# Summing the four classes of a long convolution's products on GpSimd in f32, so that an inverse transform takes 16 matmuls in place of 32

## The chip, the cores and the metric

The kernel runs on one core of a Trainium2 chip. The metric is the device time of one execution in microseconds (us); lower is better. A core has a matrix engine (TensorE, PE in the profile, with its weight loads as PEld), a vector engine (VectorE, DVE), a scalar engine (ScalarE, ACT), a general engine (GpSimd, POOL), and SyncE (SP), which here only issues DMA transfers. Each engine works through its own instruction queue in order; an instruction at the head that must wait holds all that stands behind it. Transfers run on 16 DMA engines. Operands lie in SBUF; matmul results lie in PSUM, which GpSimd does not read in this kernel.

## The reference, cut to what matters

Two independent halves share the kernel, and their outputs lie side by side.

```
a: for each of 64 segments of 32 rows: attention over 8 memory rows + 32 rows, 32 heads of 128,
   the memory rows of a segment come out of the segment before        (Wq, Wk, Wv, Wo: 4 x 8 MB)
b: P  = exp(dt * A * l),  l = 0..2047                                   (1024 channels, N = 128)
   K  = real(sum over n of C * P * dt * B)                              (1024 x 2048)
   Kf = rfft(K padded to 4096);  Uf = rfft(u padded to 4096)
   y  = irfft(Uf * Kf)[0:2048] + u * Dskip
output = concat(a, b)
```

The change lies in the last part of b: the product of the two spectra and the inverse transform back to 2048 points, scaled, with `u * Dskip` added.

## The kernel before, in words

Part b comes first (0 to about 642 us of the profiled execution), part a after it (to 1990 us). Part a goes through the 64 segments one after another; most of its weights lie in SBUF by then, and the rest is streamed from memory in every segment through four slots of 512 KB. Some of the resident weights are loaded while part b still runs, each when the SBUF that it takes is free; these loads are the `next(resident)` calls in part b, and they stand in SP's queue between the loads of part b.

Up to about 420 us, part b makes the filter K (exponentials, sines, products) and transforms the input u forward. The rows of K go through memory (`Kd`). Those transfers that are left when this stage ends are issued from GpSimd's queue (`for f_ in late: f_(gp)`; the issue is at line 1063): 40 of them, and they stand in the queue ahead of all that GpSimd is given later.

Then comes the stage of the change. The 2048 points are split into four classes by their index modulo 4; the transform's matrices (cosines and sines) are 128x128 blocks. The work is cut into 16 blocks `b`: quarter `dq = b // 4` of the channels (256 each) and row block `kc = b % 4` of the frequencies. For each block:

- TensorE makes the filter's spectrum of the next block, 40 matmuls (`spectrum`, line 1207), into PSUM tiles `hps` (two for a block, three buffers from block 4 on).
- VectorE multiplies it by the input's spectrum: four instructions of 128x1024 f32 (`times_u`, line 1360), one input in SBUF and one in PSUM, into `Y` and `Z`. The two input halves `uq` (`wq` in the trace) are loaded by SP with `load_u`, each when `times_u` of the block before is through with it.
- `pointwise` then does Y -= Z and Y += Z with the parts crossed (lines 1416 and 1417) and the sum and difference of the two halves of Y (line 1419, two instructions of 128x1024, f32 in, bf16 out) into `Bt[:, kc]`. `Bt` holds all four `kc` of one quarter; it has two places, one for even and one for odd quarters.
- In blocks 0 to 2 VectorE also multiplies matrices by amplitudes (`weighted`, line 1191), before and after the four instructions of `pointwise`; the spectra of the next block wait for them.

From block 4 on, two inverse transforms of the quarter before are run behind each block (`inverses(2)`). An inverse gives 2x128 points of one class `r = c // 4` for 256 channels: for each of two output blocks, four `kc` and cosine and sine, two matmuls of 128x128 by 128x256 (line 1469), one for each half of `Bt`. That is 32. Where the class needs a half with a minus sign, the matmul takes a negated copy `mn` of its matrix `MI`, which ScalarE makes ahead of time (`negated`, line 1435). ScalarE scales the sum into `yb` (line 1484); VectorE multiplies u by Dskip and adds `yb` (lines 1489 and 1490: 128x512 bf16, two inputs in SBUF). These endings are run by `end()`, behind `times_u` of the next block. ScalarE then issues the store.

After block 15 the last quarter's eight inverses remain. Three are begun over `kc` 0 to 2 (`inverse_begin`), then all eight are ended one by one, each followed by `next(resident)`, and with the first by twelve of them.

The framework keeps the order in which each engine's instructions are written and puts in the waits: a write waits until all earlier reads of the same bytes are over. GpSimd's queue in this stage holds: the 40 issues of `Kd`; in block 2 one multiplication on 4 partitions and some small fills (lines 1550 to 1553); in block 4 the constants of part a, 36 selections (line 231) and some more; in block 10 one copy (line 1688).

Of the kernel before, what the change touches and what calls it, by code (L numbers as in the profile page):

```python
# [10 lines left out]
BF16 = mybir.dt.bfloat16  # L11
F32 = mybir.dt.float32
I32 = mybir.dt.int32
I16 = mybir.dt.int16
ALU = mybir.AluOpType
ACT = mybir.ActivationFunctionType
# [682 lines left out]
def part_b(ctx, tc, u, A_re, A_im, B_re, B_im, C_re, C_im, log_dt, Dskip, out_b, ahead, copies, residents, first_state):  # L699
# [5 lines left out]
    DH, DQ = 512, 256  # L705
    v, sc, gp, pe, sy = nc.vector, nc.scalar, nc.gpsimd, nc.tensor, nc.sync
# [46 lines left out]
    with tc.tile_pool(name="b_par", bufs=1) as par, tc.tile_pool(name="b_parh", bufs=2) as parh, \  # L753
# [112 lines left out]
        low, neg = (par.tile(sh, BF16, name=n_) for n_ in ("low", "neg"))  # L866
# [441 lines left out]
    for f in range(16):  # L1308
# [14 lines left out]
        for word in ORDER if f else FIRST:  # L1323
            nm, r = word.rstrip("'"), f - word.endswith("'")
# [26 lines left out]
    def make(kc, n):  # L1351
        for _ in range(n):
            next(made[kc])
# [3 lines left out]
    def times_u(s_, Y, Z, n_):  # L1357
        us = uq[n_].rearrange("p (a c d) -> p a c d", a=2, c=2)
        for i, t_ in ((1, Z), (0, Y)):
            v.tensor_tensor(out=t_[:, n_], in0=us[:, :, i, :].unsqueeze(2).to_broadcast([128, 2, 2, DQ]), in1=s_[n_][0], op=ALU.mult)  # L1360
# [28 lines left out]
    ctx1.close()  # L1389


    mnp = ctx.enter_context(tc.tile_pool(name="b_mn", bufs=2))
    iv = ctx.enter_context(tc.tile_pool(name="b_iv", bufs=2))
    bp = ctx.enter_context(tc.tile_pool(name="b_B", bufs=1))
    Dsk = const.tile([128, D], BF16, name="Dsk")
# [3 lines left out]
    bp0 = ctx2.enter_context(tc.tile_pool(name="b_B0", bufs=1))  # L1399
# [4 lines left out]
    MI = [pool.tile([128, 2, 2, 4, 128], BF16, name="MI", tag="MI%d" % i) for i in range(8)]  # L1404
# [3 lines left out]
    def pointwise(b, s_):  # L1408
        kc, Bt = b % 4, Bs[b // 4]
        Y, Z = (pw.tile([128, 2, 2, 2, DQ], F32, name=nm, tag=nm)[:] for nm in "yz") if b else first  # L1410
        if b:
            for n_ in range(2):
                times_u(s_, Y, Z, n_)
        yield
        Yc, Zc = (t_.rearrange("p a b c d -> p (a b) c d") for t_ in (Y, Z))
        v.tensor_tensor(out=Yc[:, :, 0, :], in0=Yc[:, :, 0, :], in1=Zc[:, :, 1, :], op=ALU.subtract)
        v.tensor_tensor(out=Yc[:, :, 1, :], in0=Yc[:, :, 1, :], in1=Zc[:, :, 0, :], op=ALU.add)
        for j, op in ((0, ALU.add), (1, ALU.subtract)):
            v.tensor_tensor(out=Bt[:, kc, j], in0=Y[:, 0], in1=Y[:, 1], op=op)

    NIV, UU = 3, 7
    unsent = []
# [4 lines left out]
        sy.dma_start(out=uu[:], in_=u_v[r][:, mc:mc + 2, DQ * dq:DQ * dq + DQ])  # L1427
        return uu

    def negated(c):  # L1430
        neg = (None, (1, 2), (0, 2), (0, 1))[c // 4]
        mn = None
        if neg:
            mn = mnp.tile([128, 2, 2, 4, 128], BF16, name="mn", tag="mn")
            sc.activation(out=mn[:, :, neg[0]:neg[1]], in_=MI[c // 2][:, :, neg[0]:neg[1]], func=ACT.Copy, scale=-1.0)
        return neg, mn

    ready = []

    def inverses(n):  # L1440

        for _ in range(n):
            dq, c = todo.pop(0)
            if not ready:
                ready.append(negated(c))
            inverse(dq, c, nxt.pop(0), *ready.pop(0))
            if len(todo) >= NIV:
                nxt.append(load_inverse(*todo[NIV - 1]))

    early = {}  # L1450

    def inverse_begin(dq, c, yp):
        ready.append(negated(c)) if len(ready) * 2 <= c else None
        early[dq, c] = yp
        products_back(yp, dq, c, *ready[c // 2], range(3))

    def products_back(yp, dq, c, neg, mn, kcs):
        r, Bt = c // 4, Bs[dq]
        j = r % 2
        for b in range(2):  # L1460
            for kc in kcs:
                if kc == 3 and b == 1 and c % 4 == 2:
                    pe.matmul(yp[:, b, :], lhsT=l4[:, r, :], rhs=w4[:, DQ * dq:DQ * dq + DQ], start=False, stop=False, skip_group_check=True)
                for cs in range(2):

                    g_cs = cs if j == 0 else 1 - cs
                    minus = neg is not None and neg[0] <= cs < neg[1]
                    for half, m_, c_ in ((0, MI[c // 2], cs), (1, mn if minus else MI[c // 2], g_cs)):
                        pe.matmul(yp[:, b, :], lhsT=m_[:, b, cs, kc, :], rhs=Bt[:, kc, j, half, c_, :], start=(kc == 0 and cs == 0 and half == 0),  # L1469
                                  stop=(kc == 3 and cs == 1 and half == 1), skip_group_check=True)  # L1470

    def inverse(dq, c, uu, neg, mn):
        r, mc = c // 4, c % 4
        d = slice(DQ * dq, DQ * dq + DQ)
        if (dq, c) in early:
            yp = early[dq, c]
            products_back(yp, dq, c, neg, mn, range(3, 4))
        else:
            yp = ps_y.tile([128, 2, DQ], F32, name="yp", tag="yp")[:]
            products_back(yp, dq, c, neg, mn, range(4))  # L1480
        if todo and not ready:
            ready.append(negated(todo[0][1]))
        yb = iv.tile([128, 2, DQ], BF16, name="yb", tag="yb", bufs=2)
        sc.activation(out=yb[:], in_=yp, func=ACT.Copy, scale=float(2.0 / PLEN))
        while unsent:
            unsent.pop(0)()

        def ending():
            v.tensor_tensor(out=uu[:], in0=uu[:], in1=Dsk[:, d].unsqueeze(1).to_broadcast([128, 2, DQ]), op=ALU.mult)
            v.tensor_tensor(out=uu[:], in0=uu[:], in1=yb[:], op=ALU.add)  # L1490
            unsent.append(lambda: sc.dma_start(out=out_v[r][:, mc:mc + 2, d], in_=uu[:]))
        endings.append(ending)
# [3 lines left out]
    def end():  # L1496
        while endings:
            endings.pop(0)()

    todo = [(dq, c) for dq in range(4) for c in range(0, 16, 2)]  # L1500
    nxt = []
    Bs = [None] * 4
# [6 lines left out]
    for b in range(16):  # L1509
        dq = b // 4  # L1510
        if b % 4 == 0:
            Bs[dq] = (bp0, bp)[dq % 2].tile([128, 4, 2, 2, 2, DQ], BF16, name="Bt", tag="B")
        points = pointwise(b, now)
        next(points)
        end()
        if b + 1 < 16:
            load_u(b + 1)
        if b == 0:
            ctx_p.close()
            ps_h = ctx_h.enter_context(tc.tile_pool(name="b_psh0", bufs=2, space=PSUM))  # L1520
        if b == 3:
            nxt = [load_inverse(*todo[n_]) for n_ in range(NIV)]
            ctx_h.close()
            ctx_f.close()
            ps_h = ctx.enter_context(tc.tile_pool(name="b_psh", bufs=3, space=PSUM))
            ps_y = ctx.enter_context(tc.tile_pool(name="b_psy", bufs=2, space=PSUM))
        if b + 1 < 16:
            now = []
            for n_ in range(2):
                if b < 3:  # L1530
                    if n_:
                        next(points, None)
                    weighted(b + 1, n_, amps[b + 1])
                now.append([ps_h.tile([128, 2, 2, DQ], F32, name="hps", tag="h")[:]])
                spectrum(b + 1, n_, [now[n_][0][:, half] for half in range(2)])
                if b == 0:
                    next(points, None)
                if b < 2:
                    make(b + 2, (9, 5)[n_])
        next(points, None)  # L1540
        if b < 4:
            for i in (2 * b, 2 * b + 1):
                sy.dma_start(out=MI[i][:], in_=MId[2 * i:2 * i + 2].rearrange("c p a k q -> p c a k q"))
        if b == 2:
            ks.append(load_k(1, k1[:, 0:2560], 0))
            rows4 = g0[0:4, 5120:6144]
            for i in range(4):
                sy.dma_start(out=rows4[i:i + 1, 0:D], in_=Kd[640:641, :])
            sy.dma_start(out=w4, in_=u[0:4, :])
            gp.tensor_tensor(out=w4, in0=rows4[:, 0:D], in1=w4, op=ALU.mult)  # L1550
            gp.memset(l4, 0.0)
            gp.memset(l4[:, :, 127:128], float(PLEN / 2))
            gp.affine_select(out=l4[:, :, 127:128], in_=l4[:, :, 127:128], compare_op=ALU.is_ge, fill=0.0, base=0, pattern=[[1, 4], [0, 1]],
                             channel_multiplier=-1)
        for _ in range({1: 2, 2: 2, 3: 1, 4: 2, 5: 2, 6: 2, 7: 1, 11: 3, 12: 3, 13: 2, 14: 3}.get(b, 0)):
            next(resident)
        if b == 4:
            state = first_state(g0[0:8, 5120:6144], iv.tile([128, 8, 24], BF16, name="xt0", bufs=1))
            next(state)
        if b == 10:  # L1560
            state.send(ps_y.tile([128, 8, 128], BF16, name="yp", tag="yp")[:, :, 0:8])
        if b >= 4:
            inverses(2)
# [166 lines left out]
```

## Time and profile before

| what | value |
|---|---|
| time, median of three runs | 1983.08 us (1977.25 to 1986.69) |
| the profiled execution's own time | 1991.66 us |
| its span, first to last instruction | 1989.9 us (1.8 us lie around it) |
| TensorE busy | 1846.9 us, 93% of the span |
| VectorE busy | 1370.6 us, 69% |
| ScalarE busy | 949.3 us, 48% |
| GpSimd busy | 411.1 us, 21% |
| moved by DMA | 588.70 MB, mean 296 GB/s |
| mean granted TensorE clock | 0.973 of full |

The profiled execution is 8.6 us (0.4%) slower than the median of the three timed runs. Shares of busy time are means over the whole span, and the stage of the change is only 220 us of it (422 to 642 us), so the stage has to be read by itself: the views for it are the busy time by stretches, the timeline of one engine, the groups of one line or tile, and the chain of waits. In the timeline a row gives the start, the length, the engine, the line, the operation, the tiles written and read, the shapes, and how many instructions were merged into it. In the view of busy time by stretches each row gives the stretch, its length, the busy us (and number of instructions) of PE, PEld, DVE, ACT and POOL, the granted clock, the busy share of the DMA engines and GB/s. Rows of PE are pipelined: one matmul of 128x256 is shown with 273 ns, but the next one starts 0.109 us after it, so its rate is read from a merged row.

### The profile page before, as it was taken

What the parts mean: (1) busy time and instruction counts of PE and PEld (TensorE: products, weight loads), DVE (VectorE), ACT (ScalarE), POOL (GpSimd) and SP (SyncE); (2) the same over time, 40 slices, a digit from 0 to 9 for tenths busy, and PEclk for the clock granted to TensorE, in tenths of its full rate; (3) what the DMA queues carried; (4) which work ended last, traced back from release to release, by engine and by line L of the source; (5) the groups of instructions that cost most, each with busy time, mean ns of one, the idle gap of its engine ahead of it and who ended that gap; (6) DMA issues with size and microseconds to landing.
All of it is one profiled execution on the core that took longest, in us unless ns stands there. A gap on an engine that the chain in (4) does not pass through costs nothing.

```text
span 1989.9 us, 74737 instructions
## 1 busy us (share of the span) xinstructions
PE 1846.9 (93%) x32044; PEld 1134.5 (57%) x32044; DVE 1370.6 (69%) x3399; ACT 949.3 (48%) x1678; POOL 411.1 (21%) x859
## 2 busy tenths in 40 slices
PE   8799999778999799999999999999999999999999
PEld 3566666446887355555555555555555555555554
DVE  8499999858994466666666676666666666666650
ACT  8599999841223344343444444444444343434330
POOL 2254535224000111111111111111121111111120
PEclk9899999868999799999999999999999999999999
DMA  7789888757578899999999999999999999999991
GB/s 223 207 239 272 238 242 256 199 152 249 179 226 297 311 345 319 340 345 324 346 344 347 347 343 341 342 340 339 338 338 348 338 341 352 331 334 343 333 345 39
DMA packets 329350, 588.70 MB, mean 296 GB/s; under 512 B 86830, under 2 KB 202990, under 8 KB 326970
## 3 DMA queue, kind: packets, MB, share of 16 engines
q1 hardware_dynamic: 275592, 529.03, 78.3%
q10 hardware_dynamic: 45682, 29.82, 4.9%
q0 software_dynamic: 7744, 25.07, 3.5%
q8 instruction: 251, 4.11, 0.8%
q14 instruction: 81, 0.66, 0.1%
HBM read 528.25 MB, written 66.05 MB: 299 GB/s over the span
## 4 chain that ended last, share of the span: by engine, by line
PE 37%; DMA 24%; DVE 3%; issue 1%; ACT 1%; POOL 0%; ACTq 0%; POOLq 0%; SPq 0%; DVEq 0%
PE acc L404 20%; DMA wst<-WD_v 10%; PE pp L517 8%; DMA wst<-WD_o 6%; DMA wst<-WD_k 4%; DMA arena<-PKd 3%; PE pe L654 3%; PE tr L415 2%; DMA wst<-WD_q 1%; PE pv L485 1%; PE pv L489 1%; DVE arena L611 1%; PE sc L429 1%; ACT arena L611 1%; DVE arena L470 1%
## 5 line engine op out<-in xcount | busy, mean ns | idle before, releaser
L404 PEld LDWEIGHTS <-a_hT 128*32 128x32 bf16 x12352 | 329.7, 96 | 316.7 <-issue 62.6
L410 ACT CAST arena<-acc 128x512 bf16<-128x512 f32 x384 | 224.7, 585 | 402.0 <-PE acc L404 324.6
L517 PEld LDWEIGHTS <-arena 128*32 128x32 bf16 x8256 | 216.8, 97 | 86.3 <-issue 62.6
L404 PE MATMUL acc<-wst,a_hT 128*32 128x512 bf16 x2304 | 229.4, 382 | 26.0 <-DMA wst<-WD_v 17.6
L418 POOL COPY arena<-arena 128x128 bf16<-128x128 bf16 x128 | 37.3, 292 | 839.2 <-DMA arena<-PKd 278.6
L325 DVE TENSOR_SCALAR arena<-keep 128x256 int32<-128x256 int32 (+1 forms) x512 | 175.7, 395 | 31.5 <-PE acc L404 30.9
L404 PE MATMUL acc<-XM,a_hT 128*32 128x512 bf16 x2560 | 185.8, 381 | 0.0
L517 PE MATMUL pp<-W_o,arena 128*32 128x256 bf16 x3584 | 123.4, 274 | 6.9 <-DMA W_o<-in_A_Wo_dram 6.3
L444 DVE TENSOR_REDUCE a_mx<-sc 128x4 f32<-128x160 f32 (+1 forms) x192 | 71.6, 373 | 78.8 <-PE sc L432 78.8
L197 PE MATMUL pro<-XM,wsl 128*128 128x512 bf16 x512 | 122.3, 382 | 3.8 <-DVE kst L206 2.2
L448 ACT ACTIVATE sc<-sc 128x160 f32<-128x160 f32 (+1 forms) x192 | 63.9, 333 | 124.2 <-DVE sc L445 123.9
L404 PE MATMUL acc<-W,a_hT 128*32 128x512 bf16 x1536 | 118.6, 381 | 0.0
L532 DVE COPY arena<-tr 128x512 bf16<-128x512 bf16 x64 | 27.2, 425 | 127.7 <-PE tr L415 127.7
L452 DVE TENSOR_REDUCE a_mx<-sc 128x4 f32<-128x160 f32 (+1 forms) x192 | 72.9, 379 | 55.3 <-ACT sc L448 54.9
L1252 DVE TENSOR_SCALAR nr<-ptt 128x456 f32<-128x456 int16 x128 | 80.4, 628 | 38.6 <-PE ptt L1230 35.5
L1469 PE MATMUL yp<-Bt,MI 128*128 128x256 bf16 x680 | 104.5, 273 | 0.0
L404 PE MATMUL acc<-g,a_hT 128*32 128x512 bf16 x1024 | 101.8, 380 | 0.0
L479 POOL TENSOR_TENSOR arena<-arena,a_BD 128x128 bf16<-128x128 bf16 x128 | 51.0, 399 | 229.7 <-DVE arena L462 222.7
L1244 ACT ACTIVATE E<-pa 128x648 bf16<-128x648 f32 x128 | 87.9, 713 | 16.8 <-PE pa L1236 14.2
L611 ACT CAST arena<-pp 128x128 bf16<-128x128 f32 x64 | 17.0, 265 | 164.7 <-DVE arena L611 164.7
L404 PE MATMUL acc<-wq,a_hT 128*32 128x512 bf16 x1024 | 90.8, 382 | 0.0
L517 PE MATMUL pp<-wst,arena 128*32 128x256 bf16 x1536 | 76.5, 275 | 15.2 <-DMA wst<-WD_o 13.1
(332 smaller groups left out, 4048.3 us busy)
## 6 DMA issues: line engine op xcount, KB each, us to landing
wst<-WD_v SPq DMA_DIRECT2D x256, 512.0 KB
wst<-WD_k SPq DMA_DIRECT2D x192, 512.0 KB
wst<-WD_o SPq DMA_DIRECT2D x192, 512.0 KB
wst<-WD_q SPq DMA_DIRECT2D x128, 512.0 KB
Ud<-ux POOLq DMA_DIRECT2D x16, 1024.0 KB, 7.9
wq<-Ud SPq DMA_DIRECT2D x32, 512.0 KB
wsl<-in_A_Wk_dram SPq DMA_DIRECT2D x16, 512.0 KB
wsl<-in_A_Wv_dram SPq DMA_DIRECT2D x16, 512.0 KB
```

Source lines behind the costliest of these rows:

```text
L197: nc.tensor.matmul(a[:], lhsT=w[:, kc, 128 * j:128 * j + 128], rhs=xTl[:, kc, :, :].rearrange("p s k -> p (s k)"), start=(kc == 0), stop=( ...
L325: nc.vector.tensor_scalar(out=out.bitcast(I32), in0=in_.bitcast(I32), scalar1=0, scalar2=None, op0=ALU.bitwise_or)
L404: nc.tensor.matmul(a[32 * g:32 * g + 32, o_:o_ + rhs.shape[1]], lhsT=hT[:, kc, :], rhs=rhs, start=(kc == 0), stop=(kc == KC - 1), tile_pos ...
L410: nc.scalar.copy(out=q, in_=a[:])
L444: nc.vector.tensor_reduce(out=m_, in_=x, axis=AX.X, op=ALU.max)
L448: nc.scalar.activation(out=flat(sc, i), in_=flat(sc, i), func=ACT.Exp, scale=scale)
L452: nc.vector.tensor_reduce(out=m_, in_=x, axis=AX.X, op=ALU.add)
L517: nc.tensor.matmul(po[32 * qt:32 * qt + 32, o_:o_ + rhs.shape[1]], lhsT=oT[:, h % 4, (h % 16) // 4, :], rhs=rhs, start=False, stop=(h == 3 ...
L654: nc.tensor.matmul(pe[n][:], lhsT=left[2 * b + hi // 16][:, 128 * (hi % 16):128 * (hi % 16) + 128], rhs=wo[u][:, 1024 * hh + 512 * n:1024 ...
L1244: sc.activation(out=T["E", r, e // 4][:, lo:lo + 8 * NE].rearrange("p (i c) -> p i c", i=2), in_=T.pop(("p", r, e))[:, :, 0:4 * NE], func= ...
L1252: v.tensor_scalar(out=T["n", r, e // 4][:, lo:lo + 8 * NT], in0=T.pop(("t", r, e))[:, 0:8 * NT].bitcast(I16)[:, 0:16 * NT:2], scalar1=floa ...
L1469: pe.matmul(yp[:, b, :], lhsT=m_[:, b, cs, kc, :], rhs=Bt[:, kc, j, half, c_, :], start=(kc == 0 and cs == 0 and half == 0), stop=(kc == 3 ...
```

## The change

VectorE now writes the sum and the difference of Y's halves in f32 into one tile `halves_` (8 KB a partition, one buffer, in the place where the two negated matrices lay). GpSimd makes the four classes from it with four instructions of 128x512 (f32 in, bf16 out) for each block: the first two read the sum, the last two the difference, one operand of each of these with its two rows in reverse order. `Bt` has the same size and is now indexed by class and part. An inverse takes two matmuls where it took four, 16 in all, and no negated matrix. All that ScalarE did for `mn` is gone. Nothing else is moved.

```diff
-    mnp = ctx.enter_context(tc.tile_pool(name="b_mn", bufs=2))
+    clp = ctx.enter_context(tc.tile_pool(name="b_cl", bufs=1))
+    halves_ = clp.tile([128, 2, 2, 2, DQ], F32, name="hv")
...
+        X = halves_
         for j, op in ((0, ALU.add), (1, ALU.subtract)):
-            v.tensor_tensor(out=Bt[:, kc, j], in0=Y[:, 0], in1=Y[:, 1], op=op)
+            v.tensor_tensor(out=X[:, j], in0=Y[:, 0], in1=Y[:, 1], op=op)
+        for r, op in ((0, ALU.add), (2, ALU.subtract)):
+            gp.tensor_tensor(out=Bt[:, kc, 2 * r:2 * r + 2], in0=X[:, 0, 0], in1=X[:, 0, 1], op=op)
+        gp.tensor_tensor(out=Bt[:, kc, 2:8:5], in0=X[:, 1, 0], in1=X[:, 1, 1, ::-1], op=ALU.add)
+        gp.tensor_tensor(out=Bt[:, kc, 3:7:3], in0=X[:, 1, 0, ::-1], in1=X[:, 1, 1], op=ALU.subtract)
...
-    def negated(c):
-        neg = (None, (1, 2), (0, 2), (0, 1))[c // 4]
...
-            sc.activation(out=mn[:, :, neg[0]:neg[1]], in_=MI[c // 2][:, :, neg[0]:neg[1]], func=ACT.Copy, scale=-1.0)
...
                 for cs in range(2):
-
-                    g_cs = cs if j == 0 else 1 - cs
-                    minus = neg is not None and neg[0] <= cs < neg[1]
-                    for half, m_, c_ in ((0, MI[c // 2], cs), (1, mn if minus else MI[c // 2], g_cs)):
-                        pe.matmul(yp[:, b, :], lhsT=m_[:, b, cs, kc, :], rhs=Bt[:, kc, j, half, c_, :], start=(kc == 0 and cs == 0 and half == 0),
-                                  stop=(kc == 3 and cs == 1 and half == 1), skip_group_check=True)
+                    pe.matmul(yp[:, b, :], lhsT=MI[c // 2][:, b, cs, kc, :], rhs=Bt[:, kc, 2 * r + cs, :], start=(kc == 0 and cs == 0),
+                              stop=(kc == 3 and cs == 1), skip_group_check=True)
...
-            Bs[dq] = (bp0, bp)[dq % 2].tile([128, 4, 2, 2, 2, DQ], BF16, name="Bt", tag="B")
+            Bs[dq] = (bp0, bp)[dq % 2].tile([128, 4, 8, DQ], BF16, name="Bt", tag="B")
```

More of the change, by code (lines that the diff above doesn't have):

```diff
@@ L1428, in load_inverse @@
         return uu
-    def negated(c):
-        neg = (None, (1, 2), (0, 2), (0, 1))[c // 4]
-        mn = None
-        if neg:
-            mn = mnp.tile([128, 2, 2, 4, 128], BF16, name="mn", tag="mn")
-            sc.activation(out=mn[:, :, neg[0]:neg[1]], in_=MI[c // 2][:, :, neg[0]:neg[1]], func=ACT.Copy, scale=-1.0)
-        return neg, mn
-    ready = []
     def inverses(n):
@@ L1443, in inverses @@
             dq, c = todo.pop(0)
-            if not ready:
-                ready.append(negated(c))
-            inverse(dq, c, nxt.pop(0), *ready.pop(0))
+            inverse(dq, c, nxt.pop(0))
             if len(todo) >= NIV:
@@ L1452, in inverse_begin, with products_back @@
     def inverse_begin(dq, c, yp):
-        ready.append(negated(c)) if len(ready) * 2 <= c else None
         early[dq, c] = yp
-        products_back(yp, dq, c, *ready[c // 2], range(3))
-    def products_back(yp, dq, c, neg, mn, kcs):
+        products_back(yp, dq, c, range(3))
+    def products_back(yp, dq, c, kcs):
         r, Bt = c // 4, Bs[dq]
-        j = r % 2
         for b in range(2):
@@ L1464, in products_back, with inverse @@
                 for cs in range(2):
-                    g_cs = cs if j == 0 else 1 - cs
-                    minus = neg is not None and neg[0] <= cs < neg[1]
-                    for half, m_, c_ in ((0, MI[c // 2], cs), (1, mn if minus else MI[c // 2], g_cs)):
-                        pe.matmul(yp[:, b, :], lhsT=m_[:, b, cs, kc, :], rhs=Bt[:, kc, j, half, c_, :], start=(kc == 0 and cs == 0 and half == 0),
-                                  stop=(kc == 3 and cs == 1 and half == 1), skip_group_check=True)
-    def inverse(dq, c, uu, neg, mn):
+                    pe.matmul(yp[:, b, :], lhsT=MI[c // 2][:, b, cs, kc, :], rhs=Bt[:, kc, 2 * r + cs, :], start=(kc == 0 and cs == 0),
+                              stop=(kc == 3 and cs == 1), skip_group_check=True)
+    def inverse(dq, c, uu):
         r, mc = c // 4, c % 4
@@ L1476, in inverse @@
             yp = early[dq, c]
-            products_back(yp, dq, c, neg, mn, range(3, 4))
+            products_back(yp, dq, c, range(3, 4))
         else:
             yp = ps_y.tile([128, 2, DQ], F32, name="yp", tag="yp")[:]
-            products_back(yp, dq, c, neg, mn, range(4))
-        if todo and not ready:
-            ready.append(negated(todo[0][1]))
+            products_back(yp, dq, c, range(4))
         yb = iv.tile([128, 2, DQ], BF16, name="yb", tag="yb", bufs=2)
```

## The prediction

> **What bounds the kernel now.** First the page, for the size of the stage. It has 1024 matmuls of line 1469 (680+248+88+8 in the groups). Then the busy time by stretches (stretch, us, PE, PEld, DVE, ACT, POOL, clock, DMA share, GB/s):
>
> ```profile
> 475.00:500.00 25.00, 25.00 (x227) 21.84 (x226) 24.48 (x27) 7.99 (x8) 9.01 (x28) 1.00 0.86 277
> 575.00:608.00 33.00, 33.00 (x299) 28.64 (x296) 29.99 (x36) 11.40 (x13) 0.00 (x0) 1.00 0.71 215
> 608.00:622.00 14.00, 12.80 (x113) 10.63 (x112) 3.05 (x9) 4.35 (x7) 0.00 (x0) 1.00 0.98 349
> 622.00:642.00 20.00, 19.29 (x185) 15.39 (x182) 5.48 (x13) 8.48 (x9) 0.00 (x0) 1.00 0.99 323
> ```
>
> To be seen: up to 608 PE is full, but DVE is at 91 to 98% beside it; from 608 PE is nearly full, and DMA is full as well. Next, one block's timeline of DVE, with PE's row beside it:
>
> ```profile
> 523.31 2.36 DVE L1419 TENSOR_TENSOR Bt<-y 128x1024 bf16<-128x1024 f32 x2
> 525.59 1.22 DVE L1360 TENSOR_TENSOR z<-wq,hps 128x1024 f32<-128x1024 f32 x1
> ...
> 530.11 0.42 DVE L1489 TENSOR_TENSOR uu<-uu,Dsk 128x512 bf16<-128x512 bf16 x1
> ...
> 531.93 0.43 DVE L1490 TENSOR_TENSOR uu<-uu,yb 128x512 bf16<-128x512 bf16 x1 [0.53 <-ACT yb L1484]
> 532.28 1.22 DVE L1416 TENSOR_TENSOR y<-y,z 128x1024 f32<-128x1024 f32 x1
> ```
> ```profile
> 523.74 6.71 PE L1469 MATMUL yp<-Bt,MI 128*128 128x256 bf16 x60
> ```
>
> A matmul takes (6.71-0.27)/59 = 0.109 us. The starts of line 1416 are 10.93 us apart in the first four blocks (477.11 to 520.85), where DVE never waits, and 11.69 in the next seven (to 602.69), where it waits about 0.5 to 0.9 for `yb`, so for PE. The mean is 125.58/11 = 11.42. DVE's own floor is 10.93: halving PE's part cannot take more than 0.5 us from a block.
>
> Last, GpSimd's queue, which gets new work, and how its work goes together with DVE's:
>
> ```profile
> 420.24 1.77 POOL L1063 DMA_DIRECT2D Kd<-KxT  x3 [34.59 <-ACT XM L1160]
> ...
> 442.65 0.55 POOL L1063 DMA_DIRECT2D Kd<-KxT  x1 [2.34 <-issue]
> ...
> 458.59 1.07 POOL L1063 DMA_DIRECT2D Kd<-KxT  x2 [0.64 <-issue]
> 466.95 2.22 POOL L1550 TENSOR_TENSOR k<-g,k 4x1024 bf16<-4x1024 bf16 x1 [7.28 <-DMA k<-in_B_u_dram]
> ...
> 471.72 12.07 POOL L231 TENSOR_SCALAR_AFFINE_SELECT a_mask<-a_mask 32x24 bf16<-32x24 bf16 x36
> ```
> ```profile
> L992 POOL TENSOR_TENSOR ux<-us x16: 1257/1263/1272, 87.5 to 380.1; 128x512 f32<-128x512 f32 x16
> ```
> ```profile
> L1419 DVE TENSOR_TENSOR Bt<-y x30: 1211/1222/3024, 441.0 to 606.2; 128x1024 bf16<-128x1024 f32 x30
> ```
>
> To be seen: GpSimd issues `Kd` until 459.7 and makes part a's constants from 470.3 to 485.0. The one instruction of line 1419 that took 3024 ns instead of 1222 is the one that began at 467.23, while GpSimd's 1550 ran to 469.17. So a DVE instruction with two SBUF inputs and a GpSimd instruction shut each other out. Those with one input in PSUM don't: line 1021 takes 679 to 683 ns beside GpSimd's 991 to 994.
>
> **The change, part by part.**
>
> *Removed.* 512 matmuls x 0.109 = 55.8 us of PE: 41.9 up to 608, hidden behind DVE's floor as above, and 14.0 after it. 24 negations on ScalarE (1.05 or 1.91 us each), idle over half of the stage; PE waited 1.3 us for them in all, which lies in the tail. DVE keeps its count; f32 out costs no more than bf16 (line 1416 1219 ns, line 1419 1222).
>
> *Added: GpSimd's 64 instructions.* No such one (512 elements, f32 in, bf16 out) is in the trace. Line 992 (f32 out) has 1263 ns and starts 1.2 us after its twin 991; line 900 (1024 elements, bf16 out) has 2126 at best, so 1063 for half. A reversed operand is not shown; double would be the upper end. I take 1.2, since 992 has the shape: 4.9 us for four, 4.3 to 5.1 without the reversal.
>
> *Step 1, the wait at block 1.* The halves have one buffer. GpSimd's four for block 0 stand behind the 40 issues of `Kd`. DVE comes to the sum of block 1 at 441.0, and may write only when GpSimd has read block 0's sum. The issues ended at 459.7. From 441 on DVE stands, SP's next loads wait for it, and the DMA engines have less to do. At the bare 0.55 us the 19 issues left at 442.65 would end at 453.5. I take the middle, 457, since the rows show both bursts at that pace and gaps. Then 4 x 1.22 for GpSimd (462) and 2.3 for DVE's two: 464.2, where before it was 443.4. That is +20.8 (17.4 to 23.6). Queued behind it on DVE: `weighted` of block 2, so PE's spectra, then all blocks to 15. From there to the first product of block 4 (472.46 before, 29.1 us) DVE has about 22 us of own work, up to 2 us for the spectrum of block 2, and the 6.5 us that the load of block 4 takes from its issue, of which some 2 stand out; together 26. So 3 us come back: **+18** (14 to 22).
>
> *Step 2, the constants.* They follow block 4's classes on GpSimd. Alone a selection takes 0.18 us, one each 0.25; against DVE's two-input instructions only one gets through for each (four of 1.07 to 1.24 us between 477.1 and 481.9). They end some 20 to 23 us after block 4's difference, and block 5's classes come after them; DVE wants to write block 6's sum at 20.7. **+5** (3 to 7).
>
> *Step 3, the blocks' period.* GpSimd's four begin when DVE's difference ends, run beside `times_u` (no clash), and end 5.0 us later (4.4 to 5.2). DVE comes to line 1489 after 4.44 and waits 0.56 (0 to 0.7). Period 11.5 (10.93 to 11.65) against 11.42, over 11 periods: **+1** (-5 to +3).
>
> *Step 4, the tail.* Block 15's difference ended at 607.4, PE's last matmul of the stage at 639.4: 32 us. Now PE waits 5 us for GpSimd, and has 92 matmuls left (10 us) and some 1.7 more at a lower clock: 17 us, 15 less. But the loads for part a cannot start sooner (their places come free with that difference), and DMA is full from 608 on:
>
> ```profile
> 640.00:650.00 10.00, 5.54 (x72) 2.48 (x65) 4.46 (x11) 1.40 (x3) 0.21 (x1) 0.98 0.97 334
> 650.00:660.00 10.00, 9.05 (x165) 4.33 (x158) 4.98 (x12) 5.54 (x10) 1.49 (x5) 0.85 0.80 256
> 660.00:670.00 10.00, 6.15 (x120) 3.41 (x112) 6.09 (x21) 2.27 (x6) 1.29 (x3) 0.83 0.96 354
> 670.00:680.00 10.00, 4.80 (x68) 2.30 (x64) 0.47 (x2) 0.56 (x3) 0.00 (x0) 0.50 0.97 357
> ```
>
> The PE that came early would stand still here; it already did, 25.5 of 40 us busy. Only DMA's gaps can be filled: 2.0 us at 650, 2.3 at 680 to 690 (share 0.77). **-4** (-8 to 0).
>
> *Sum:* 18+5+1-4 = +20 on the profiled 1991.7, so about 2012 there. The median lies 8.6 lower: 1983.1+20 = **2003**. The terms' bounds add up to +4 and +32; together they hardly fall that way, and I take +12 to +28 for this case, 1995 to 2011.
>
> **The rivals.**
>
> *A, not slower: `Kd` gets out in time.* Place: GpSimd's queue from 420 to 442. If the gaps between the issues (17.0 us of idle in all, 22.1 busy) are due to DVE and not to the transfers, the issues could end at 420.2+22.1 = 442.3, and the sum of block 1 waits 4 instead of 20 us. From step 1 +1 is left: 1+5+1-4 = +3, **1986**, within 0.5%. It decides from an end of the issues before about 446; each us later costs one. Against it: the longest gap (4.27 us to 432.23) has DVE idle for 2.5 of it and DMA nearly full. 0.14. [...]
>
> *B, faster: PE was the bound all through.* If GpSimd's work clashed with nothing, the queue let it by, and part a could start when PE is done, the gain would be 5 in the periods and 15 in the tail: -20, **1963**. For it: PE's 25.00 of 25. Against: DVE's floor, DMA's 0.98. 0.06.
>
> *C, slower still: the clock.* PE would have 72 matmuls, 7.9 us, in 11.5, with a gap of some 3.6. Gaps bring the clock down here: from 451.6 to 455.0 PE was busy 2.01 of 3.40, and the next 3.4 us had clock 0.50. If it stayed there, 72 x 0.218 = 15.7 us a block: +4.2 x 11 on top, **2049**. Against: 472.0 to 475.4 had 1.78 busy and clock 1.00 after it, and one low window of 3.4 us adds 1.7 to 7.9, still under 11.5. 0.04. [...]
>
> *D, slower still: reversed rows cost double.* Two of the four at 2.4: 7.3 us, so DVE waits 2.9 at line 1489, 2.4 more x 11 = +26, **2029**. Nothing in the trace shows it. 0.08.
>
> **How the numbers follow.** Forecast 0.68, A 0.14, B 0.06, C 0.04, D 0.08. 0.5% (about what a measurement of this kernel can tell from no change) is 9.9 us: faster 0.06, same 0.14, slower 0.80. The range takes in A and the forecast and leaves out B, C and most of D: 1984 to 2021.
>
> **What would show it.** A wait of some 19 us of DVE at the new sum in block 1, ended by GpSimd; a second of a few us two blocks after the constants; line 1489 waiting about half a us for GpSimd in each block; PE with gaps in the blocks, and low clock in some windows; the last matmul of the stage 17 us after the last difference; DMA full and PE waiting behind it. It is wrong if GpSimd's `Kd` ends near 442, if GpSimd's four take far from 5 us, or if part a's first segment starts earlier than DMA lets it in this forecast.

## The result, and the profile after

The changed kernel takes 2007.3 us (median; 2004.44 to 2014.13 in six runs) beside 1983.53 for the kernel before (1977.25 to 1988.87, six runs). The ratio is 1.0128 with a 95% interval of 1.0101 to 1.0155: slower, by 20 to 31 us. The prediction was 2003, in a range of 1984 to 2021.

The profiled execution of after took 2006.71 us. Its page begins:

```profile
span 2005.0 us, 73768 instructions
...
PE 1803.0 (90%) x31532; PEld 1086.9 (54%) x31532; DVE 1380.0 (69%) x3399; ACT 919.4 (46%) x1654; POOL 504.0 (25%) x923
```

PE is busy 43.9 us less than before and ACT 29.9 us less, and the time is longer: what was taken from these two did not shorten it (e5 below asks what it is worth alone). In after, lines 1417 and 1418 are Y -= Z and Y += Z, 1421 is the sum and the difference of Y's halves in f32 (`hv`), 1423 to 1425 are GpSimd's four, 1457 is the inverse's matmul, 1475 and 1476 are the endings. The busy time by stretches (columns as in the prediction) answers to the rows shown of before:

```profile
575.00:608.00 33.00, 26.70 (x219) 21.78 (x218) 32.07 (x37) 3.58 (x6) 17.35 (x14) 0.95 0.90 270
622.00:642.00 20.00, 11.30 (x68) 7.39 (x67) 15.04 (x21) 4.18 (x7) 6.88 (x5) 0.74 0.83 254
640.00:650.00 10.00, 8.03 (x82) 5.58 (x80) 0.00 (x0) 1.19 (x2) 0.00 (x0) 1.00 0.79 260
650.00:660.00 10.00, 0.00 (x0) 0.00 (x0) 3.12 (x7) 1.19 (x2) 0.00 (x0) 0.58 0.95 309
```

To be seen: in 575 to 608 PE has fallen from 33.00 of 33 to 26.70, and DVE has risen from 29.99 to 32.07. DVE is what the blocks go by now. From 650 to 660 PE does nothing at all, with DMA at 0.95.

To find the places where time came or went, take three marks in each trace: the start of line 1416's instruction in block 0 (before; 1417 after), that in block 4, that in block 15; and as an end the moment at which GpSimd's queue comes to the second wait of line 376, the copy with which it hands on to a segment of part a (693.0 us in before, 712.3 in after; the copy itself starts 2.3 and 3.0 us later). The same marks are read in each experiment (the expectation of e11 calls the last one the third segment). With that copy or the next one as the end, the differences to before change by at most 2.1 us. "Ratio" is that of the time to the kernel before on the same chip, with its interval.

| kernel | block 0 to 4 | 4 to 15 | 15 to the mark | sum | ratio |
|---|---|---|---|---|---|
| before | 54.3 | 125.6 | 90.3 | 270.2 | 1 |
| after | 71.5 | 130.7 | 88.2 | 290.4 | 1.0128 [1.0101, 1.0155] |
| e1_dve01 | 56.2 | 130.6 | 85.8 | 272.6 | 1.0007 [0.9986, 1.0027] |
| e2_dve01_const | 55.4 | 123.7 | 85.4 | 264.5 | 0.9986 [0.9965, 1.0007] |
| e3_const | 71.7 | 123.7 | 87.7 | 283.1 | 1.0089 [1.0054, 1.0124] |
| e4_all_dve | 58.1 | 146.8 | 85.8 | 290.7 | 1.0098 [1.0065, 1.0131] |
| e5_half | 54.1 | 120.4 | 87.8 | 262.4 | 0.9961 [0.9934, 0.9987] |
| e7_before_const | 54.6 | 125.6 | 90.8 | 270.9 | 1.0007 [0.9985, 1.0029] |
| e8_uu5 | 53.7 | 124.3 | 90.5 | 268.5 | 1.0008 [0.9985, 1.0030] |
| e9_kd_split | 60.4 | 130.8 | 89.7 | 280.9 | 1.0069 [1.0041, 1.0096] |
| e10_best | 55.3 | 123.7 | 93.2 | 272.3 | 1.0028 [1.0001, 1.0055] |
| e11_uu_act | 56.7 | 123.6 | 85.4 | 265.7 | 1.0004 [0.9983, 1.0025] |
| e13_before_uu_act | 56.6 | 128.0 | 94.6 | 279.2 | 1.0060 [1.0033, 1.0087] |

After against before, from the marks before rounding: +17.3, +5.2 and -2.2, so +20.3 at the mark. What follows the mark, the rest of part a, is the same instructions in all thirteen kernels, and took anything from 1282.0 to 1303.9 us in their profiled executions (before 1296.9, after 1292.7). A span of one execution is therefore no measure here, and the two columns at the right are read together: the sum says where, the ratio says how much. They agree within 6 us in every row (e3: +12.9 at the mark, 0.89% or 17.7 us in the time).

**Block 1.** DVE's timeline, then GpSimd's (start, length, then what it waited for in brackets):

```profile
457.74 4.62 DVE L1421 TENSOR_TENSOR hv<-y 128x1024 f32<-128x1024 f32 x2 [18.01 <-POOL Bt L1423]
462.29 2.01 DVE L1191 TENSOR_TENSOR XM<-XM,wq 128x1536 bf16<-128x1536 bf16 x1
```
```profile
439.51 0.55 POOL L1063 DMA_DIRECT2D Kd<-KxT  x1 [0.81 <-issue]
444.07 6.36 POOL L1063 DMA_DIRECT2D Kd<-KxT  x11 [4.00 <-issue]
451.43 3.78 POOL L1063 DMA_DIRECT2D Kd<-KxT  x7 [0.99 <-issue]
455.22 2.49 POOL L1423 TENSOR_TENSOR Bt<-hv 128x512 bf16<-128x512 f32 x2
457.66 1.26 POOL L1424 TENSOR_TENSOR Bt<-hv 128x512 bf16<-128x512 f32 x1
458.88 1.25 POOL L1425 TENSOR_TENSOR Bt<-hv 128x512 bf16<-128x512 f32 x1
```

The same two places of DVE in before, and then all of line 1421 in after (shortest, median and longest in ns):

```profile
441.00 2.36 DVE L1419 TENSOR_TENSOR Bt<-y 128x1024 bf16<-128x1024 f32 x2
443.28 0.95 DVE L1191 TENSOR_TENSOR XM<-XM,wq 128x1536 bf16<-128x1536 bf16 x1
```
```profile
L1421 DVE TENSOR_TENSOR hv<-y x30: 1211/1225/3483, 457.7 to 627.7; 128x1024 f32<-128x1024 f32 x30
```

To be seen: block 0's classes could start only when the last `Kd` was issued, at 455.21, though their input was ready at 426.5. DVE stood from 439.7 to 457.7 for them. It goes on when the sum has been read, not when all four are through; but its two then take 4.62 us instead of 2.36. The first of them is the longest of its line, 3.48 us: it runs beside 1424 and 1425 and ends 1.1 us behind them (461.2 against 460.1). The next instruction, `weighted`, takes 2.01 instead of 0.95, beside block 1's classes (line 1423, from 461.31 on).

**The constants**, GpSimd's timeline and DVE's:

```profile
503.83 14.84 POOL L231 TENSOR_SCALAR_AFFINE_SELECT a_mask<-a_mask 32x24 bf16<-32x24 bf16 x36
...
519.85 2.49 POOL L1423 TENSOR_TENSOR Bt<-hv 128x512 bf16<-128x512 f32 x2
```
```profile
522.37 2.27 DVE L1421 TENSOR_TENSOR hv<-y 128x1024 f32<-128x1024 f32 x1 [4.28 <-POOL Bt L1423]
...
525.79 2.27 DVE L1421 TENSOR_TENSOR hv<-y 128x1024 f32<-128x1024 f32 x1 [1.15 <-POOL Bt L1425]
```

Block 5's classes stand behind the 36 selections, and block 6's sum and difference behind those classes. One period between blocks is 18.49 us, where those after it are 11.22 to 11.24.

**A block in the steady state**, DVE and GpSimd:

```profile
604.08 2.36 DVE L1421 TENSOR_TENSOR hv<-y 128x1024 f32<-128x1024 f32 x2
...
610.88 0.66 DVE L1475 TENSOR_TENSOR uu<-uu,Dsk 128x512 bf16<-128x512 bf16 x1
```
```profile
605.38 3.41 POOL L1423 TENSOR_TENSOR Bt<-hv 128x512 bf16<-128x512 f32 x2 [5.35 <-DVE hv L1421]
608.75 1.27 POOL L1424 TENSOR_TENSOR Bt<-hv 128x512 bf16<-128x512 f32 x1
609.99 1.27 POOL L1425 TENSOR_TENSOR Bt<-hv 128x512 bf16<-128x512 f32 x1
```

The sum and difference end at 606.44; GpSimd's four end at 611.26, 4.8 us later, and line 1475 stretches from 0.42 to 0.66 beside the last of them.

**The tail**, DVE's timeline:

```profile
654.70 0.42 DVE L1475 TENSOR_TENSOR uu<-uu,Dsk 128x512 bf16<-128x512 bf16 x1 [14.95 <-DMA uu<-in_B_u_dram]
```

and PE's:

```profile
661.71 1.40 PE L404 MATMUL acc<-arena,a_hT 128*32 128x512 bf16 x4 [12.36 <-DVE arena L325]
```

PE's last inverse matmul ended at 646.2, 17.3 us after the last difference; before it was 32.2. What comes next is late: a row of u arrives at 654.7, and PE stands from 649.4 to 661.7. It waits for weights of part a that VectorE unpacks (line 325), and in VectorE's queue line 325 stands behind endings that wait for that row.

### The profile page after: what moved, and what is told of

It is laid out like the page before. It is cut to its first block, busy times and chain, and to the rows that moved or that the text cites. A ratio compares the mean times of both kernels' runs of the same rounds, so it can differ in the third digit from the quotient of the medians.

```text
span 2005.0 us, 73768 instructions
## 1 busy us (share of the span) xinstructions
PE 1803.0 (90%) x31532; PEld 1086.9 (54%) x31532; DVE 1380.0 (69%) x3399; ACT 919.4 (46%) x1654; POOL 504.0 (25%) x923
## 4 chain that ended last, share of the span: by engine, by line
PE 37%; DMA 25%; DVE 3%; ACT 1%; issue 1%; POOL 0%; ACTq 0%; SPq 0%; POOLq 0%; DVEq 0%
PE acc L404 21%; DMA wst<-WD_v 10%; DMA wst<-WD_o 8%; PE pp L517 8%; PE pe L654 3%; DMA arena<-PKd 2%; PE tr L415 2%; DMA wst<-WD_k 2%; DMA wst<-WD_q 2%; PE pv L485 1%; DVE arena L611 1%; PE pv L489 1%; PE sc L429 1%; ACT arena L611 1%; PE tro L617 1%
## 5 line engine op out<-in xcount | busy, mean ns | idle before, releaser
L452 DVE TENSOR_REDUCE a_mx<-sc 128x4 f32<-128x160 f32 (+1 forms) x192 | 72.9, 380 | 55.4 <-ACT sc L448 55.0
L1244 ACT ACTIVATE E<-pa 128x648 bf16<-128x648 f32 x128 | 88.0, 714 | 15.8 <-PE pa L1236 13.7
L1470 ACT ACTIVATE yb<-yp 128x512 bf16<-128x512 f32 x29 | 17.3, 597 | 159.2 <-PE yp L1457 132.6
```

The source lines that it names most:

```text
L452: nc.vector.tensor_reduce(out=m_, in_=x, axis=AX.X, op=ALU.add)
L1244: sc.activation(out=T["E", r, e // 4][:, lo:lo + 8 * NE].rearrange("p (i c) -> p i c", i=2), in_=T.pop(("p", r, e))[:, :, 0:4 * NE], func= ...
```

## The experiments

The theory after the result, **Q**: the loss is two waits in GpSimd's queue, one behind the issues of `Kd` and one behind the constants, and the classes in the other blocks cost nothing. Its rival, **L**: GpSimd's instructions and DVE's shut each other out in every block, and that is the loss. For the tail, **D**: DMA is full, so PE's early end buys little; the rival, **U**: the tail goes by the loads of u's rows (where they stand in a queue, or how early they are asked for; the expectations of e11 and e13 call it S).

**e1_dve01**: the first wait taken away, by giving GpSimd nothing to do in blocks 0 and 1.

```diff
+        eng = v if b < 2 else gp
...
-            gp.tensor_tensor(out=Bt[:, kc, 2 * r:2 * r + 2], in0=X[:, 0, 0], in1=X[:, 0, 1], op=op)
+            eng.tensor_tensor(out=Bt[:, kc, 2 * r:2 * r + 2], in0=X[:, 0, 0], in1=X[:, 0, 1], op=op)
```

> The changed kernel with the classes of blocks 0 and 1 summed by VectorE, all other blocks by GpSimd. Theory Q (the loss is waiting in GpSimd's queue: 17 us at block 1 behind the issues of Kd, 7 us at block 6 behind part a's constants): the wait of 18 us before block 1's sum is gone, VectorE has 8 x 0.6 = 4.9 us more, about half of it in its waits for PE: 2007 - 17 + 3 = 1993. Theory L (the loss is GpSimd's sums and their clashes with VectorE in every block): 2 of 16 blocks, so an eighth of 24: 2004.

Measured: 1.0007 [0.9986, 1.0027]; 17.8 us less at the mark than after. DVE's timeline, in block 1 and in block 6:

```profile
441.83 2.36 DVE L1421 TENSOR_TENSOR hv<-y 128x1024 f32<-128x1024 f32 x2
444.11 1.29 DVE L1424 TENSOR_TENSOR Bt<-hv 128x512 bf16<-128x512 f32 x2
...
508.75 2.27 DVE L1421 TENSOR_TENSOR hv<-y 128x1024 f32<-128x1024 f32 x1 [4.26 <-POOL Bt L1424]
```

The sum begins at once and in block 6 the second wait is as before. Moving 2 of 16 blocks takes nearly the whole loss away, while GpSimd goes on beside DVE in the other 14. That speaks for Q and against L. The expectation, 1993 us, is a ratio of 1.0048 and lies above the interval: at the mark the gain has the size that Q gives it, in the time it is larger, by no more than the two columns differ elsewhere.

**e2_dve01_const**: e1, and the second wait taken away too: the constants are made ahead of the `Kd` issues.

```diff
+    constants(tc, ahead)
     for f_ in late:
         f_(gp)
...
-        hT = constants(tc, ahead)
+        hT = ahead.low["hT"]
```

> As the run with blocks 0 and 1 on VectorE, and part a's constants put ahead of the issues of Kd in GpSimd's queue, where it stands idle for 34 us. Theory Q: the wait of 7 us at block 6 goes too: 1993 - 7 = 1986, so within 0.3% of the kernel before. Theory L: 2004, as without this edit.

Measured: 0.9986 [0.9965, 1.0007], not to be told from before. GpSimd's timeline shows the selections in what had been its idle time:

```profile
388.02 12.93 POOL L231 TENSOR_SCALAR_AFFINE_SELECT a_mask<-a_mask 32x24 bf16<-32x24 bf16 x36
```

All periods from block 5 on are now 11.22 to 11.24, and the time up to the mark is 26.0 us shorter than after's, 5.7 shorter than before's. Both waits are the loss; this is the best version of the change that was found.

**e3_const**: after, with the early constants alone. The diff is the one of e2, without e1's.

> The changed kernel with part a's constants put ahead of the issues of Kd, and nothing else: GpSimd sums all blocks. Theory Q (two separate waits in GpSimd's queue): block 6's wait of 7 us goes, block 1's stays: ratio to the kernel before 1.0128 less 0.0035, so 1.009. Rival (the second wait is only the first one's late effect): both waits stay, 1.0128.

Measured: 1.0089 [1.0054, 1.0124]; 7.3 us less at the mark than after. Block 1 waits 18.15 us in its timeline, as in after, and the long period is gone (11.23 us where after has 18.49). The intervals of the two times overlap, so it is the trace that tells them apart. 17.8 (e1) and 7.3 (e3) add up to 25.1, against the 26.0 of both together: the two waits are separate terms.

**e7_before_const**, the control: the early constants in the kernel before.

> The kernel before with part a's constants put ahead of the issues of Kd. GpSimd holds nothing that another engine waits for in that stage, so no theory expects anything: ratio 1.000 (0.998 to 1.002). If it is faster by 0.3%, the gain of the constants' move in the other runs says nothing on the wait.

Measured: 1.0007 [0.9985, 1.0029], +0.7 at the mark. The constants cost nothing where they are in before, and gain nothing by the move; they became a term only by GpSimd's new work behind them.

**e4_all_dve**: after, with all classes on VectorE (`eng = v` in e1's diff), so GpSimd has no part in it.

> The changed kernel with all sums on VectorE, none on GpSimd. Theory Q: no wait for GpSimd anywhere, but VectorE has 4 x 0.6 = 2.4 us more in a block: period 13.3 instead of 11.42 x 11 = +21, about +4 in blocks 0 to 3, -2 in the tail: 1983.5 + 23 = 2006, the same time as the changed kernel's by another way. Theory L: without GpSimd the clashes are gone, and it is clearly faster than the changed kernel, 1995 or less.

Measured: 1.0098 [1.0065, 1.0131]. DVE's timeline, two starts of one line in neighbouring blocks:

```profile
561.14 1.22 DVE L1417 TENSOR_TENSOR y<-y,z 128x1024 f32<-128x1024 f32 x1
...
574.56 1.22 DVE L1417 TENSOR_TENSOR y<-y,z 128x1024 f32<-128x1024 f32 x1
```

The period is 13.33 in most blocks (13.42 here), with four sums at 0.60 us each. That is 2.1 more than with GpSimd in each of the eleven periods: 23 us (146.8 against 123.7 in e2). GpSimd's sums, 1.27 us each, are better placed there than 0.60 on DVE, which has no room. So GpSimd's classes beside DVE are the cheaper way in the steady state, which is against L once more.

**e5_half**: how much PE's work was worth, by itself: the kernel before, with the second half's matmuls and the negations left out.

```diff
-                    for half, m_, c_ in ((0, MI[c // 2], cs), (1, mn if minus else MI[c // 2], g_cs)):
+                    for half, m_, c_ in ((0, MI[c // 2], cs),):
...
-            sc.activation(out=mn[:, :, neg[0]:neg[1]], in_=MI[c // 2][:, :, neg[0]:neg[1]], func=ACT.Copy, scale=-1.0)
```

> The kernel before with the matmuls of the second half of Bt and the negated matrices left out (so half of each inverse's products is missing): what the halving of the matmuls is worth alone, with nothing added. Theory of the prediction (VectorE's floor of 10.93 us a block, and a tail that ends by loads and not by PE): 5 in the blocks and 1 to 4 in the tail, 1983.5 - 8 = 1975. Rival B (PE is the bound all through): 5 and 14: 1964.

Measured: 0.9961 [0.9934, 0.9987], 7.8 us less at the mark: 5.1 in blocks 4 to 15, 2.5 after. The busy time by stretches:

```profile
550.00:575.00 25.00, 21.41 (x175) 17.26 (x173) 24.34 (x29) 2.98 (x5) 0.00 (x0) 0.93 0.92 280
...
620.00:630.00 10.00, 2.15 (x23) 0.54 (x12) 4.11 (x10) 1.19 (x2) 0.00 (x0) 0.67 1.04 376
```

In the blocks DVE is at 97%, and the periods are 10.92 to 11.02, the floor of DVE that the prediction gave; in the tail PE is busy 2.15 of 10 with DMA full. So 512 matmuls and 24 negations less, with nothing put in their place, are worth 8 us. In this kernel, halving PE's matmuls could not have given the 20 us of rival B.

**e9_kd_split**: the first wait made shorter in another way: every other issue of `Kd` goes to SP.

```diff
-    for f_ in late:
-        f_(gp)
+    for n_, f_ in enumerate(late):
+        f_((sy, gp)[n_ % 2])
```

> The changed kernel with every other one of the 40 issues of Kd given to SP; the classes stay on GpSimd. Theory Q: GpSimd's queue is free some 16 us sooner (about 439), the wait before block 1's sum shrinks from 18 us to 3 or less; SP is held some 8 to 10 us longer, and as much of it as the loads for block 1 are late comes back. Ratio to the kernel before 1.004 to 1.008 instead of 1.0128. Rival (the loss does not hang on that queue): 1.0128.

Measured: 1.0069 [1.0041, 1.0096]; 9.5 us less at the mark than after. GpSimd's timeline and then DVE's in block 1:

```profile
438.79 2.49 POOL L1423 TENSOR_TENSOR Bt<-hv 128x512 bf16<-128x512 f32 x2
```
```profile
442.46 1.22 DVE L1360 TENSOR_TENSOR z<-wq,hps 128x1024 f32<-128x1024 f32 x1 [12.41 <-DMA wq<-Ud]
...
450.31 2.36 DVE L1421 TENSOR_TENSOR hv<-y 128x1024 f32<-128x1024 f32 x2
```

Block 0's classes start 16.4 us earlier than in after (455.22), and block 1's sum waits for nothing. But from block 0 to 1 it takes 23.4 us where it took 15.6 in after and 15.8 in before: DVE waits 12.41 us for block 1's input, whose loads now stand behind twenty issues in SP's queue (issued at 436.6, where after has 423.6). The queue's length is the cause, and it moved along with the issues; e1, which moves the work out of the queue, gains 8 us more.

**e8_uu5**: the tail. e2, with the rows of u asked for five inverses ahead instead of three (`NIV, UU = 5, 7`).

> The run with blocks 0 and 1 on VectorE and the constants early, and in addition the rows of u for the inverses loaded five inverses ahead instead of three (NIV 5), so that fewer of them stand in SP's queue behind twelve loads of weights. Theory D (after the last difference DMA is full and decides when part a gets on): same as without it, ratio 0.9986, within 0.002. Theory U (the tail waits for those rows, 11.8 us of VectorE before the sixth ending): the first segment starts earlier and 4 to 6 us come back, ratio 0.996.

Measured: 1.0008 [0.9985, 1.0030]; from the last difference to the mark 85.7 us, where e2 has 80.6. The waits of SP's queue from 590 to 690 (us in all, times, longest), and one stretch:

```profile
SPq L1435 <- DMA out_dram<-uu: 21.8, 5, 9.2
```
```profile
600.00:610.00 10.00, 3.13 (x22) 2.04 (x19) 9.69 (x10) 1.79 (x3) 5.03 (x4) 0.72 0.29 82
```

With seven buffers, loads five ahead want a place whose store hasn't landed; SP stands (21.8 us in all, where e2 has 10.9), and with it all weights behind: DMA's share is 0.29, where e2 has 0.70. U expected a gain here, and D none: neither expected this loss of 5 us. It shows only that SP's queue is easily made worse.

**e10_best**: e8, and the classes of block 15 on VectorE as well, to have PE begin the last inverses sooner (`eng = v if b < 2 or b == 15 else gp`).

> As the run with NIV 5, and block 15's classes summed by VectorE too, which has nothing else to do then: 4 x 0.6 us instead of 6.4 us of GpSimd, so PE goes on 4 us earlier. Theory D: still no more, ratio 0.9986. Theory U: 4 us more on top, ratio 0.994.

Measured: 1.0028 [1.0001, 1.0055]; 88.4 us from the last difference to the mark. PE ended 16.7 us after the difference instead of 17.1 in e8, where 4 us had been expected: its wait for ScalarE's scaling (line 1472) grew from 1.36 to 2.41 us. Why it is a little worse than e8 was not found.

**e11_uu_act** and **e13_before_uu_act**: U in another form. The rows of u are loaded from ScalarE's queue, so that they stand behind no weights; in e2 and in before.

```diff
-        sy.dma_start(out=uu[:], in_=u_v[r][:, mc:mc + 2, DQ * dq:DQ * dq + DQ])
+        sc.dma_start(out=uu[:], in_=u_v[r][:, mc:mc + 2, DQ * dq:DQ * dq + DQ])
```

> The run with blocks 0 and 1 on VectorE and the constants early, with the rows of u for the inverses loaded from ScalarE's queue instead of SP's (three ahead as before), so that no load of weights stands behind a wait for one of their buffers. Theory D (from the last difference on DMA is full): the tail from that difference to the third segment stays at 80.6 us, at most 3 less; ratio 0.998. Theory S (SP's order holds up the weights): 5 us or more come back, ratio 0.995 or less.

> The kernel before with the rows of u for the inverses loaded from ScalarE's queue. Theory D: no change, 1.000 (0.998 to 1.002). Theory S: the waits in SP's queue are there in the kernel before as well, so it gains too, 0.996 to 0.998.

Measured: e11 1.0004 [0.9983, 1.0025], and 80.6 us from the last difference to the mark, just as e2. That is D's number. The waits of VectorE from 606 to 690, in e2 and then in e11 (us in all, times, longest), show that the rows did come earlier:

```profile
DVE uu L1477 <- DMA uu<-in_B_u_dram: 12.9, 3, 11.8
...
DVE keep L325 <- DMA wst<-in_A_Wq_dram: 6.7, 1, 6.7
```
```profile
DVE keep L325 <- DMA wst<-in_A_Wq_dram: 14.7, 1, 14.7
...
DVE uu L1477 <- DMA uu<-in_B_u_dram: 5.7, 3, 2.9
```

What the rows gave up, a load of part a's weights took: it ended VectorE's wait at 644.6 us in e2 and at 645.3 in e11. SP issued it at 638.7 and 638.1, behind the other weights, and DMA's share was 1.00 to 1.03 from 620 to 640 in both. So the waits for rows of u are not what the tail goes by.

e13 1.0060 [1.0033, 1.0087], which neither theory expected: 9.0 us more at the mark, and 89.9 us instead of 85.6 from the last difference on. Its waits from 600 to 660 say a part of why:

```profile
PE yp L1469 <- ACT mn L1435: 4.4, 2, 3.3
```

In before, ScalarE also makes the negated matrices; these now stand behind the loads, which themselves wait for places, and PE waits for them, 4.4 us where it was 1.3 in before (its last inverse matmul came 38.9 us after the difference instead of 32.2; what makes the rest of this delay is not shown). The changed kernel has no negations, so e11 doesn't show it. The move is a loss in the one and nothing in the other.

## Why the prediction was right, point by point

**Step 1, +18: right (+17.3).** Against the start of its own stage, block 4's first product came 17.3 us later. `Kd` ended at 455.21, where 457 was taken. From there to the end of block 1's difference it was 7.1 us as against 7.2, but not as worked out: DVE's sum waited for two of GpSimd's four and not for all, and then its two took 4.62 instead of 2.3, because the sum was held up beside the other two. Two errors that cancel, by luck. Block 1's difference ended 20.0 us later than in before, and 2.8 of them had come back by block 4 (3 were said). The rows have the 4.62 for 2.36, and the 2.01 for 0.95 of line 1191, beside GpSimd's classes; by what the one holds up the other is not shown. **Rival A** (`Kd` gets out by 442) is out: 455.2. Its condition, gaps between the issues that are due to DVE, is not met by the longest of them in after either: its 4.00 us up to 444.07 lie where DVE stands. What the issues wait for in the gaps is not shown. In e9 the queue was free at 438.8 with half of the issues, and only then was the wait gone.

**Step 2, +5: right in kind, too small.** It measured +7.3 (18.49 - 11.23), just over the 3 to 7 allowed; e3 took 7.3 away. The end of the constants was as taken: 519.9, which is 21.6 after block 4's difference (20 to 23 were said). The mis-sized term is what DVE does behind them. It wanted to write the sum at 518.1 and waited 4.28; but then sum and difference each took 2.27 instead of some 1.2 beside GpSimd's classes, and the difference waited another 1.15 for line 1425. 4.28 + 1.15 + 2 x 1.05 = 7.5, and the prediction had counted the first of the three and little more.

**Step 3, +1: somewhat too high (-2.1).** The period is 11.23 instead of 11.5. GpSimd's four end 4.8 us after the difference, where 5.0 was taken (the first starts behind the sum already, and runs beside the difference), and DVE loses 0.24 instead of 0.56 at the ending. 11 x (11.23 - 11.42) = -2.1, inside the -5 to +3. **Rival D** is out by the row of line 1424, whose second operand has its rows in reverse order:

```profile
L1424 POOL TENSOR_TENSOR Bt<-hv x16: 1257/1267/1438, 457.7 to 631.4; 128x512 bf16<-128x512 f32 x16
```

1267 ns at the median, as line 992's 1263 without a reversal. **Rival C**, the clock, did come about, in single windows; the busy time by stretches of 3.4 us:

```profile
549.30:552.70 3.40, 0.51 (x5) 0.22 (x4) 3.40 (x4) 0.00 (x0) 3.40 (x3) 1.00 0.02 5
552.70:556.10 3.40, 3.40 (x17) 2.42 (x18) 3.30 (x5) 0.00 (x0) 2.40 (x2) 0.50 0.48 180
556.10:559.50 3.40, 3.40 (x33) 3.05 (x32) 3.19 (x5) 0.60 (x1) 0.00 (x0) 1.00 0.70 215
```

Half the clock in one window, 17 matmuls instead of 33, the full one in the next, and a period of 11.23 all the same: PE has room in it. In the blocks of period 11.23 there are two low windows (clock 0.50 from 552.7 to 556.1 and from 586.8 to 590.2), each single, behind windows with PE busy for 0.51 and 0.60 us of 3.40. Not all low windows are single: where PE stood for the second wait, the clock was 0.50 from 525.4 to 535.6. After how little work of PE a low window comes is not shown: in the prediction's rows 2.01 us busy of 3.40 were followed by half the clock, and 1.78 were not.

**Step 4, -4: right in kind, half as large (-2.2, within the -8 to 0).** PE ended 17.3 us after the last difference (17 was said, 15 less than before), and 2.2 of the 15 arrived at the mark. That the transfers decide was the reason given. e5 bears it out (2.5 us of gain for half of the inverse's matmuls), and so does e11, where the rows of u came earlier and a load of weights took over the wait. The runs do not show what would make the tail shorter: e8 and e10, which were to, made it longer. That DMA is the only limit there is not shown: its share was 0.54 from 620 to 630 and 0.79 from 640 to 650 in after, and e1 and e2, without the two waits, have a tail 2.4 to 2.8 us shorter than after's. What these gaps wait for stays open.

**Rival B**, PE as the bound, is out by e5: half of the inverse's matmuls and all negations gone, and 7.8 us at the mark.

**The sum.** At the mark +20.3, and +20 was predicted; the errors of the steps were -0.7, +2.3, -3.1 and +1.8, and cancel: that the sum is this close is luck. The range of 1984 to 2021 takes in rival A, so that the time fell into it says little alone; what bears the prediction out is that both waits were there, and that each went when its cause was taken away. The median moved by 23.8, 3.5 more than the sum. With a rest of part a that varies by 22 us from execution to execution, and an interval of the ratio that begins at +20.0, that is no difference that asks for a cause.

## What to carry to other kernels

Work that is moved to an idle engine has to be looked at in that engine's queue: here 36 us of transfer issues and 17 us of constants, which had held up other engines by 0.2 us at most in before, became 25 us because one buffer lay between them and VectorE. An engine that is busy all the time need not be the bound while another is nearly full beside it: leave its work out (e5) before you pay anything for shortening it. Two edits of a few lines (e1 and e3) took back the loss, each the amount of its own wait, and what the change is worth without the waits, 5.7 us at the mark, cannot be told from nothing in the time.

## What the runs showed of the hardware that was not expected

- The same instructions of part a, from the mark to the end, took 1282.0 to 1303.9 us in thirteen profiled executions, 1.7% apart, with DMA near its full share (0.96 from 684 to 1940 us in after). Whole runs of one kernel are as far apart: before took 1976.61 to 1998.35 us in 25 runs on one chip.
- GpSimd's 36 small selections took 12.07 us beside DVE's instructions in before, 14.84 in after and 12.93 when moved to 388 us. Most take 0.18 us and start 0.25 us apart; the rest of the time lies in a few of up to 1.26 us, in before and after beside VectorE's instructions with two inputs in SBUF.
- A queue of transfers can be made slow by asking earlier: with rows of u five instead of three ahead and the same seven buffers, SP waited 21.8 us for stores to land, and DMA's share fell to 0.29 for 10 us.
